# Attention, two feed-forward networks, one core: the first group of tokens becomes the first 192 of both batches

## The chip, the cores and the metric

The kernel runs on 1 core of one Trainium2 chip. Its engines are TensorE (PE, with its weight loads listed apart as PEld), VectorE (DVE), ScalarE (ACT), GpSimd (POOL) and SyncE (SP), whose queue issues all DMAs here. The metric is the device time of one execution in microseconds; the median of several runs counts. A change of about half a per cent is the least that is told apart.

## The reference, cut to what matters

```python
B, H, S, D = (2, 8, 576, 64)
scores = q @ k.T / sqrt(D), causal; a = softmax(scores); local = a @ v
q_p = where(q > 0, q, exp(q) - 1) + 1
mem_out = (q_p @ M_prev) / (q_p . z_prev + 1e-6)
x = g * mem_out + (1 - g) * local            # 1152 tokens (b, s) of 512
x = elu(x @ w_in) @ w_out                    # 512 -> 2048 -> 512
out = sum_e p[:, e] * (relu(x @ w1[e]) @ w2[e])   # 4 experts, 512 -> 1024 -> 512
```

All is float32. The weights of the first network come as float64.

## The kernel before, in words

Products of 32-bit accuracy are made of three matmuls on parts: each operand is split in a high part (ACT) and a low part (its remainder, POOL or DVE), and high x high, high x low and low x high are summed in PSUM (`mm3`, lines 249 to 252).

The 1152 tokens go through the two networks in two groups. Group 0 has 384 tokens (`NTOK`, line 254 on), group 1 has 768 and a second scheme with fewer products (`Wide`, line 661), which needs four differences of token quarters, T1 to T4 (`Halves.plan`, lines 630 to 658): a subtraction on DVE, a high part on ACT (`high`), a low part on POOL (`low`, L651), each in two halves kk. This is done twice: on the attention's output x ahead of the first network of group 1, and on its result y ahead of the second. Both are called junctions below.

Attention comes in 16 units, one per batch b, part and pair of heads c (`plan_unit`, line 1026). Part A has the query tiles from 64 to 448, which see 192, 320 and 448 keys; part B the tile from 448 to 576, which sees all 576, and the first 64 queries, doubled to fill a tile. A unit loads queries and keys, splits them (`split_h` on ACT, `split_l` on POOL, L1057), makes phi(q) for the memory part (`phi_r`, `phi_e` on ACT, `phi_p`, `phi` on POOL), and multiplies it with the memory (`mem`, L1108, one product per tile and head into bank o). The scores of the two heads are made side by side, in 64 rows of the array each (`score`, L1146, six matmuls for one piece of keys); DVE masks them, negates and finds the lowest (`lowest`, L1154); ACT makes the exponentials; 128 x 128 blocks are turned on PE (`transposes`, L1202), copied out of PSUM by ACT or DVE in turn (`evac`, L1208 and L1210) and multiplied with the values (`values`, L1217 for a full block, L1224 for the diagonal half blocks of both heads). DVE scales both parts (`quotient`, `times`, L1089 and L1095), POOL adds them (`both`, L1256), PE turns the sum (`turn`, L1262), and ACT and DVE write its parts to x (`join`, L1271 and L1273) or a plain copy (`join_w`, L1276).

The order on every engine is written out ahead by a planner (`Plan.order`, line 955): each step has an engine, an assumed cost, a rank (when it is due, in assumed us), steps it comes after, and buffers that it takes and gives back. A free engine takes the ready step of lowest rank. There are 13 matmuls on zeros first, to fill the time of the first loads (`WARM`). The four units 0A of group 0 are due 5 us apart; the layers' clock starts at `START2` = 60; the other twelve units are due at `START2` plus the entries of `STARTS2`, and run beside the networks of group 0:

```python
    GATE = ("0A3", "score10")
    START2 = 60.0
    STARTS2 = [30, 66, 74, 86, 97, 108, 119, 130, 141, 152, 163, 174]
    units = [(b, part, c) for b, part in ((0, "B"), (1, "A"), (1, "B")) for c in range(H // 2)]
```

The first network's 16 weight tiles arrive as float64 and are made float32 beside it (`plan_weights`, line 161): per half of a tile ACT scales the upper words into a PSUM bank s0 or s1 (`upper`, L193), and DVE shifts, joins and signs in three passes over 512 columns (L197, L201, L207). These two banks are those that the scores of all units use, so `upper` waits for `GATE`, a score of the last of the units 0A. Then the tile is split (L217 on ACT, L221 on POOL) and kept in DRAM for group 1.

Of the kernel before, what the change touches and what calls it, by code (L numbers as in the profile page):

```python
# [20 lines left out]
P = 128  # L21
NPART = 4
Q0 = [0, 64, 192, 320, 448]

QR = [128] * 5
EXT = [64, 192, 320, 448, 576]


PARTS = "AB"
TILES = {"A": [3, 2, 1], "B": [4, 0]}  # L30
KEYS = {"A": 448, "B": 576}
QCOLS = {"A": 384, "B": 256}
TCOLS = {"A": 384, "B": 192}
QCOL = {"A": {1: 0, 2: 128, 3: 256}, "B": {4: 0, 0: 128}}
FULL = {"A": 3, "B": 4}

BLOCKS = {
    part: [b for i in tiles for b in [(i, odd, j) for odd in (0, 1) for j in range(i)] + [(i, 2, i)]]
    for part, tiles in TILES.items()
}  # L40
# [3 lines left out]
ROWS = [[(0, 64 + P * t, P)] for t in range(3)] + [  # L44
    [(0, 448, P)],
    [(0, 0, D), (D, S + 448, D)],
    [(0, S + 512, D), (D, S, D)],
] + [[(0, S + 64 + P * t, P)] for t in range(3)]
TOKENS = {(0, "A"): (0, 0), (0, "B"): (1, 0), (1, "B"): (1, 192), (1, "A"): (1, 384)}
# [7 lines left out]
def tile_kernel(  # L57
    ctx: ExitStack,
    tc: tile.TileContext,
    qk_a: bass.AP,  # L60
    qk_b: bass.AP,
    vm_a: bass.AP,
    vm_b: bass.AP,
# [7 lines left out]
    qk, vm = {"A": qk_a, "B": qk_b}, {"A": vm_a, "B": vm_b}  # L71
# [21 lines left out]
    zeros = const.tile([P, 512], mybir.dt.bfloat16, name="zeros")  # L93
# [25 lines left out]
    def setup_probs():  # L119
# [9 lines left out]
    W_STEP = 6.0  # L129
    W_FIRST = 5  # L130
    NW = 5
    SLOTS = {
        "raw": 2, "rv": 2, "qh": 2, "ql": 2, "pe": 1, "pp": 2, "pt": 2, "nm": 4, "nr": 4, "tm": 2, "tv": 1,
# [27 lines left out]
    def plan_weights(plan, i, rank):  # L161
# [62 lines left out]
        if k < NW1 and not second:  # L224
            ends = []
            for half in range(2):
                last[0] = None
                add(f"load{half}", "sync", 1.6, lambda half=half: load64(half), [f"w64_{half}"])
                plan.add(
                    ("w", i, f"upper{half}"), "act", act_cost(512), rank, lambda half=half: upper(half),  # L230
                    [last[0], GATE] + [("w", i, "upper0")] * half, [f"s{half}"] + ["wr"] * (half == 0),
# [7 lines left out]
                    [f"w64_{half}", f"s{half}"],  # L239
# [47 lines left out]
    class Moe1:  # L287
# [26 lines left out]
        def before_up(self, part, fc):  # L314
            if part or self.g:
                return [], []
            return [(f"0A{c}", "join_l") for c in range(H // 2)], []
# [27 lines left out]
        def act(self, key, t, n):  # L345
            def exp():
                ev = hp[0].tile([P, 512], F32, tag="ev", name="ev" + "".join(map(str, key)), bufs=SLOTS["ev"])
                t["ev"] = ev[:, :n]
                nc.scalar.activation(out=t["ev"], in_=t["ps"], func=AF.Exp)
# [253 lines left out]
    class Halves:  # L603
# [26 lines left out]
        def plan(self, plan, rank, ready):  # L630

            for name, x, y in (("T1", "B12", "B11"), ("T2", "B22", "T1"), ("T3", "B22", "B12"), ("T4", "B21", "T2")):
                for kk in (0, 1):
# [16 lines left out]
                    def low(name=name, kk=kk):  # L650
                        nc.gpsimd.tensor_tensor(  # L651
# [7 lines left out]
                    plan.add(key(name, "l"), "pool", pool_cost(384), rank, low, [key(name, "h")], [], ["t32"] * kk)  # L659
# [278 lines left out]
    class Plan:  # L938
# [4 lines left out]
        def __init__(self, slots):  # L943
            self.steps, self.slots = {}, slots

        def add(self, key, engine, cost, rank, fn, after=(), takes=(), gives=(), slack=0.0):


            self.steps[key] = (engine, cost, rank, fn, after, takes, list(gives), slack)

# [4 lines left out]
        def order(self, free=None):  # L955
# [32 lines left out]
            while any(queues.values()):  # L988
# [27 lines left out]
                if not moved:  # L1016
                    times = [x + y for x in (*free.values(), *ends.values()) for y in slacks if x + y > now]
                    assert times, f"no step can start: {[q[:3] for q in queues.values()]}, {rings}"
# [4 lines left out]
    def segments(i):  # L1023
        return [(0, EXT[i])] if EXT[i] <= 512 else [(0, 288), (288, 576)]

    def plan_unit(plan, b, part, c, start, spare, slack):

        tiles, nt, nq, nk = TILES[part], len(TILES[part]), QCOLS[part], KEYS[part]
        slot = {i: n for n, i in enumerate(tiles)}
        base = {i: sum(EXT[x] for x in tiles[:n]) for n, i in enumerate(tiles)}  # L1030
        width = sum(EXT[i] for i in tiles)
        widest, entries = 960, 2 * FULL["B"] + 3
        unit, uid = {}, f"{b}{part}{c}"

        def add(key, engine, cost, fn, after=(), takes=(), gives=()):
            kind = key.rstrip("0123456789")
            plan.add(
                (uid, key), engine, cost, start + OFFSET[kind], fn,
                [(uid, a) if isinstance(a, str) else a for a in after], takes, gives, slack.get(engine, 0.0),
            )  # L1040


        def load():
            unit["k"] = atile([P, KEYS["A"] + QCOLS["A"]], F32, tag="raw", name=f"qk{uid}")[:, :nq + nk]
            nc.sync.dma_start(out=unit["k"], in_=qk[part][b, c])

        def load_v():
            unit["rv"] = atile([P, entries, DV], F32, tag="rv", name=f"rv{uid}")[:, :2 * FULL[part] + nt + 1]
            nc.sync.dma_start(out=unit["rv"], in_=vm[part][b, c])
# [351 lines left out]
```

## Time and profile before

| what | value |
|---|---|
| median of 3 runs | 754.3 us (753.38 to 756.7) |
| the profiled execution | 756.79 us |
| its span, first to last instruction | 755.0 us |
| PE busy | 730.8 us, 97% of the span |
| DVE, ACT, POOL busy | 422.7, 363.2, 443.9 us |
| mean granted clock of TensorE | 0.975 |

Matmuls overlap in the records: one of 384 columns is told as 0.34 us long, and the next starts after half of that. So the distance between starts, not the length, tells what PE can do. In a row of the timeline a first number is the start, the second the time from the first start to the last end; "x12" counts the instructions in it, and the bracket tells how long the engine was idle before, and what ended that.

### The profile page before, as it was taken

The page shows a single profiled execution, that of the slowest core. Times are in us where ns is not written, and L with a number is a line of the kernel's source. Part 1 is how long each engine was busy: PE and PEld are TensorE (multiplying, and loading weights), DVE is VectorE, ACT ScalarE, POOL GpSimd, SP SyncE. Part 2 cuts the span into 40 slices and gives each one's busy share as a digit, 9 for nine tenths or more (in the row PEclk, how much of TensorE's full clock was granted, in tenths as well). Part 3 has the DMA queues.
Part 4 walks back from the last instruction along what each step waited for, and adds up shares of the span by engine and source line. Part 5 has one row for each costly group of instructions (what it writes and reads, how often), then busy time and mean ns, then how long its engine had stood idle before and what let it go on. Part 6 is the DMA issues. An engine that isn't in the chain of part 4 may idle for free.

```text
span 755.0 us, 11115 instructions
## 1 busy us (share of the span) xinstructions
PE 730.8 (97%) x4205; PEld 656.1 (87%) x4205; DVE 422.7 (56%) x919; ACT 363.2 (48%) x639; POOL 443.9 (59%) x273
## 2 busy tenths in 40 slices
PE   9979898999999999999899999979999999999997
PEld 5868798888888888888799999969989889899896
DVE  4588879634534444443663674885546355364562
ACT  5657856855444354453475573853333234232220
POOL 5646656885574375454998655676456565665210
PEclk9968989999999999999899999989999999999999
DMA  6249878664253342330232131202213122032002
GB/s 239 82 142 317 285 237 269 216 210 118 75 154 92 102 127 66 113 113 29 99 100 94 63 107 50 63 28 85 84 29 111 37 77 84 28 112 56 1 0 84
DMA packets 24709, 82.61 MB, mean 109 GB/s; under 512 B 3024, under 2 KB 3024, under 8 KB 24656
## 3 DMA queue, kind: packets, MB, share of 16 engines
q1 hardware_dynamic: 24656, 81.91, 34.4%
q8 instruction: 33, 0.54, 0.3%
q14 instruction: 20, 0.16, 0.1%
HBM read 71.15 MB, written 10.75 MB: 108 GB/s over the span
## 4 chain that ended last, share of the span: by engine, by line
PE 85%; DVE 8%; ACT 2%; issue 2%; POOL 2%; DMA 1%; SPq 0%; DVEq 0%; POOLq 0%; ACTq 0%
PE db L250 9%; PE db L252 9%; PE db L251 9%; PE ub L250 4%; PE da L250 3%; PE da L252 3%; PE da L251 3%; PE ub L252 3%; PE ub L251 3%; PE o0A L1217 2%; DVE cv L201 2%; DVE cv L197 2%; PE o1A L1217 1%; DVE wr L207 1%; DVE yT L642 1%
## 5 line engine op out<-in xcount | busy, mean ns | idle before, releaser
L221 POOL TENSOR_TENSOR wl<-wr,wh 128x1024 fp32r<-128x1024 f32 x72 | 171.9, 2395 | 128.1 <-ACT wh L217 125.8
L217 ACT ACTIVATE wh<-wr 128x1024 fp32r<-128x1024 f32 x72 | 75.6, 1056 | 107.8 <-PE db L251 71.7
L250 PE MATMUL db<-wh,hb 128*128 128x512 f32 x288 | 115.8, 402 | 0.0
L252 PE MATMUL db<-wl,hb 128*128 128x512 f32 x288 | 112.8, 392 | 0.0
L251 PE MATMUL db<-wh,hb 128*128 128x512 f32 x288 | 112.6, 391 | 0.0
L899 DVE SCALAR_TENSOR_TENSOR acc<-db,pr,acc 128x512 f32<-128x512 f32 x42 | 31.5, 751 | 70.9 <-PE db L252 70.9
L250 PE MATMUL da<-ha,wh 128*128 128x384 f32 x192 | 66.1, 344 | 1.3 <-DVE xr L400 1.2
L252 PE MATMUL da<-ha,wh 128*128 128x384 f32 x192 | 65.4, 340 | 0.8 <-POOL ha L364 0.8
L251 PE MATMUL da<-ha,wl 128*128 128x384 f32 x192 | 65.1, 339 | 0.5 <-POOL wl L221 0.5
L252 PEld LDWEIGHTS db<-wl,hb 128*128 128x128 f32 x288 | 54.1, 188 | 11.8
L250 PEld LDWEIGHTS db<-wh,hb 128*128 128x128 f32 x288 | 54.1, 188 | 11.4 <-issue 0.5
L251 PEld LDWEIGHTS db<-wh,hb 128*128 128x128 f32 x288 | 54.2, 188 | 9.9
L250 PE MATMUL ub<-yh,wh 128*128 128x384 f32 x128 | 47.0, 367 | 0.0
L252 PE MATMUL ub<-yl,wh 128*128 128x384 f32 x128 | 43.2, 337 | 0.0
L251 PE MATMUL ub<-yh,wl 128*128 128x384 f32 x128 | 42.9, 335 | 0.0
L463 DVE SCALAR_TENSOR_TENSOR hb<-ub,hb 128x384 fp32r<-128x384 f32 x32 | 17.8, 556 | 38.2 <-ACT hb L460 38.1
L250 PEld LDWEIGHTS da<-ha,wh 128*128 128x128 f32 x192 | 36.6, 191 | 2.6 <-DVE xr L400 1.6
L252 PEld LDWEIGHTS da<-ha,wh 128*128 128x128 f32 x192 | 36.5, 190 | 1.9 <-POOL ha L364 1.7
L251 PEld LDWEIGHTS da<-ha,wl 128*128 128x128 f32 x192 | 36.6, 191 | 0.8 <-POOL wl L221 0.8
L460 ACT ACTIVATE hb<-ub 128x384 fp32r<-128x384 f32 x32 | 15.7, 491 | 32.9 <-PE ub L252 32.6
L490 DVE SCALAR_TENSOR_TENSOR acc<-db,pr,acc 128x512 f32<-128x512 f32 x21 | 15.7, 750 | 21.0 <-PE db L252 21.0
L250 PEld LDWEIGHTS ub<-yh,wh 128*128 128x128 f32 x128 | 24.1, 188 | 2.6 <-issue 1.5
(944 smaller groups left out, 1959.2 us busy)
## 6 DMA issues: line engine op xcount, KB each, us to landing
wr<-in_w SPq DMA_DIRECT2D x64, 512.0 KB, 3.7
w<-in_w SPq DMA_DIRECT2D x32, 512.0 KB, 5.7
wscr<-wr SPq DMA_DIRECT2D x16, 512.0 KB, 6.5
wr<-wscr SPq DMA_DIRECT2D x16, 512.0 KB, 3.4
out<-acc SPq DMA_DIRECT2D x7, 256.0 KB, 2.0
qk0A<-in_qk_a SPq DMA_DIRECT2D x4, 416.0 KB, 4.5
qk0B<-in_qk_b SPq DMA_DIRECT2D x4, 416.0 KB, 3.8
qk1A<-in_qk_a SPq DMA_DIRECT2D x4, 416.0 KB, 3.7
```

The source lines that it names most:

```text
L197: nc.vector.tensor_scalar(out=c, in0=c, scalar1=3, scalar2=None, op0=ALU.logical_shift_left)
L201: nc.vector.scalar_tensor_tensor(out=c, in0=low, scalar=29, in1=c, op0=ALU.logical_shift_right, op1=ALU.bitwise_or)
L217: nc.scalar.activation(out=t["wh"], in_=t["wr"], func=AF.Copy)
L221: nc.gpsimd.tensor_tensor(out=wl, in0=t["wr"], in1=f32(t["wh"]), op=ALU.subtract)
L250: nc.tensor.matmul(out, ah, bh, start=first, stop=False)
L251: nc.tensor.matmul(out, al, bh, start=False, stop=False)
L252: nc.tensor.matmul(out, ah, bl, start=False, stop=last)
L460: nc.scalar.activation(out=t["h"][:, 0], in_=t["ps"], func=AF.Relu)
L463: nc.vector.scalar_tensor_tensor(out=t["h"][:, 1], in0=t["ps"], scalar=0.0, in1=f32(t["h"][:, 0]), op0=ALU.max, op1=ALU.subtract)
L490: nc.vector.scalar_tensor_tensor(out=acc, in0=t["ps"], scalar=p, in1=acc, op0=ALU.mult, op1=ALU.add)
L899: nc.vector.scalar_tensor_tensor(out=acc, in0=t["ps"], scalar=p, in1=acc, op0=ALU.mult, op1=ALU.add)
L1217: nc.tensor.matmul(unit["ov"][:r, odd, slot[i]], pf[:, col:col + r], unit["rv"][:, odd * FULL[part] + (i - 1 - j if odd else j)], start=j ...
```

## The change

Group 0 is now the first 192 tokens of both batches. Attention has four units F, one for each pair of heads, for both batches: tiles 64 to 192 of batch 0 and of batch 1, which see 192 keys, and one tile that holds the first 64 queries of both batches. The scores of this third tile are two products into one bank, with zero columns in place of the other batch. F adds the two terms of phi in PSUM (two memory products) and makes max(q, 0) on ACT, so POOL has neither `phi_p` nor `phi` there; the first F unit's `split_l` is on DVE. Eight units R (batch, pair of heads) with the three tiles from 192 to 576, which see 320, 448 and 576 keys, come beside the layers, and no step of theirs may start more than 4 us ahead of its rank. The first weight tile is converted in banks m and doesn't wait for the gate. The low parts of T1 to T4 are on DVE for kk = 1. The rows of the output and of the second network's factors are ordered to match.

```diff
+QCOLS = {"F": 448, "R": 384}
+TILES = {"F": [(64, 192), (64, 192), (0, 64)], "R": [(448, 576), (320, 448), (192, 320)]}
+KEYS = {"F": 192, "R": 576}
+ROWS = [[(0, 64, P)], [(0, S + 64, P)], [(0, 0, D), (D, S, D)]] + [
+    [(0, S * b + 192 + P * t, P)] for b in (0, 1) for t in range(3)
+]
...
-    W_STEP = 6.0
+    W_RANKS = [12.0, 26.0, 32.0, 38.0, 44.0]
+    W_EARLY = 1
-        ... "tm": 2, ...
+        ... "tm": 1, ...
-    GATE = ("0A3", "score10")
+    GATE = ("F3", "score20")
+    EARLY = 4.0
-    START2 = 60.0
-    STARTS2 = [30, 66, 74, 86, 97, 108, 119, 130, 141, 152, 163, 174]
+    START2 = 48.0
+    STARTS2 = [12, 45, 75, 95, 110, 125, 140, 155]
...
-            t["cv", half] = abank(f"s{half}", f"cv{i}_{half}")
+            t["cv", half] = abank("m" if i < W_EARLY else f"s{half}", f"cv{i}_{half}")
...
-                    [last[0], GATE] + [("w", i, "upper0")] * half, [f"s{half}"] + ["wr"] * (half == 0),
+                    [last[0]] + [GATE] * (i >= W_EARLY) + [("w", i, "upper0")] * half, [bank] + ["wr"] * (half == 0),
...
                     def low(name=name, kk=kk):
-                        nc.gpsimd.tensor_tensor(
+                        eng = nc.vector if kk else nc.gpsimd
+                        eng.tensor_tensor(
...
-                        if not can_take(takes) or any(takers.get(x, [key])[0] != key for x in takes):
+                        if self.first[key] > now + 1e-6 or not can_take(takes) or any(takers.get(x, [key])[0] != key for x in takes):
...
+        def parts_of(t):
+
+            if kind == "F":
+                return [(t, 0, P)] if t < 2 else [(0, 0, D), (1, D, D)]
+            return [(0, 0, P)]
...
+            eng = nc.vector if uid == "F0" else nc.gpsimd
+            eng.tensor_tensor(out=unit["l"], in0=unit["k"], in1=f32(unit["h"]), op=ALU.subtract)
...
+            if kind == "F":
+                nc.scalar.activation(out=unit["phi"], in_=unit["k"][:, :nq], func=AF.Relu)
...
+            for t in range(nt):
+                for bi, r0, r in parts_of(t):
+                    q = qcol[t] + 2 * r0
+                    for odd in (0, 1):
+                        rows = slice(D * odd, D * odd + D)
+                        terms = ("e", "phi") if kind == "F" else ("phi",)
+                        for x in terms:
+                            nc.tensor.matmul(
+                                unit["om"][r0:r0 + r, odd, t], unit[x][rows, q:q + r],
+                                unit["rv"][rows, MEMORY[kind] + bi], start=x == terms[0], stop=x == terms[-1],
+                            )
...
         for i in range(WARM):
             ps = at["t"].tile([P, 512], F32, tag="t", name=f"warm{i}")
-            nc.tensor.matmul(ps, zeros[:, :P], zeros, start=True, stop=True)
+            nc.tensor.matmul(
+                ps.rearrange("p (n k) -> p n k", n=4), zeros, zeros.unsqueeze(1).to_broadcast([P, 4, P]), start=True, stop=True
+            )
...
         for c in range(H // 2):
-            plan_unit(plan, 0, "A", c, UNIT1 * c, True, {})
+            plan_unit(plan, "F", None, c, UNIT1 * c, True, {})
...
-        units = [(b, part, c) for b, part in ((0, "B"), (1, "A"), (1, "B")) for c in range(H // 2)]
+        units = [(b, c) for c in range(H // 2) for b in (0, 1)]
```

## Rows read from the trace of the kernel before

**Rows 1.** Stretches: length, busy us of PE, PEld, DVE, ACT, POOL, clock, DMA.

```profile
9.39:43.85 34.46, 31.99 (x291) 27.91 (x290) 22.44 (x79) 24.43 (x49) 20.50 (x16) 1.00 0.40 141
43.85:56.43 12.58, 10.49 (x54) 9.57 (x55) 10.11 (x20) 5.93 (x10) 5.76 (x6) 0.51 0.46 143
56.43:148.70 92.27, 85.06 (x475) 79.44 (x473) 76.17 (x150) 64.34 (x115) 60.63 (x39) 0.94 0.82 272
148.70:364.10 215.40, 215.40 (x1411) 184.37 (x1409) 91.10 (x275) 99.43 (x171) 124.99 (x75) 1.00 0.36 108
364.10:382.00 17.90, 15.37 (x68) 13.53 (x67) 14.81 (x20) 10.43 (x20) 16.85 (x12) 0.81 0.31 103
382.00:495.50 113.50, 113.50 (x656) 113.30 (x655) 70.44 (x138) 72.64 (x137) 79.10 (x45) 1.00 0.24 75
495.50:512.00 16.50, 12.27 (x51) 10.71 (x50) 13.02 (x19) 8.57 (x18) 12.69 (x11) 0.79 0.11 35
```

**Rows 2.** Timeline of PE among the units 0A, 30 to 45 us.

```profile
31.31 0.47 PE L1146 MATMUL s0A<-qh0A 64*128 64x448 f32 x2
...
32.10 0.89 PE L1108 MATMUL o0A<-rv0A,pp0A 64*128 64x65 f32 x12
33.20 0.55 PE L1262 MATMUL x0A<-ident,tv0A 128*128 128x128 f32 x3 [0.22 <-POOL tv0A L1256]
33.59 0.93 PE L1202 MATMUL t0A<-ident,pt0A 128*128 128x128 f32 x7
34.35 1.45 PE L1217 MATMUL o0A<-rv0A,pf0A 128*128 128x65 f32 x12
35.73 0.44 PE L1224 MATMUL o0A<-rv0A,pf0A 64*128 64x65 f32 x4
...
38.84 0.34 PE L1146 MATMUL s0A<-qh0A 64*128 64x192 f32 x2
...
39.34 1.09 PE L1202 MATMUL t0A<-ident,pt0A 128*128 128x128 f32 x8
```

**Rows 3.** Timeline of PE, a score piece of 64 columns and what follows.

```profile
91.25 0.30 PE L1146 MATMUL s0B<-qh0B 64*128 64x64 f32 x2 [2.09 <-DVE wr L207]
...
91.70 0.99 PE L1202 MATMUL t0B<-ident,pt0B 128*128 128x128 f32 x4
```

**Rows 4.** Timeline of DVE: evacuation, scores, quotient, next scores; one half tile's conversion.

```profile
31.91 0.68 DVE L1208 COPY pf0A<-t0A 128x512 f32<-128x512 f32 x1
32.51 0.61 DVE L1154 CUSTOM_DVE_ANT_0 pt0A<-s0A,mask 128x448 f32<-128x448 f32 x1
...
33.05 0.16 DVE L1089 SCALAR_TENSOR_TENSOR nm_0A<-o0A,wmem 128x6 f32<-128x6 f32 x1
...
33.95 0.61 DVE L1154 CUSTOM_DVE_ANT_0 pt0A<-s0A,mask 128x448 f32<-128x448 f32 x1
...
40.96 0.69 DVE L197 TENSOR_SCALAR cv<-cv 128x512 int32<-128x512 int32 x1
...
43.02 0.69 DVE L197 TENSOR_SCALAR cv<-cv 128x512 int32<-128x512 int32 x1
```

**Rows 5.** The stretch from the first weight conversion to the last, columns as rows 1.

```profile
40.96:137.80 96.84, 86.16 (x474) 80.00 (x474) 84.09 (x158) 64.77 (x118) 59.91 (x39) 0.88 0.76 251
```

**Rows 6.** Groups of PE's attention instructions, 56.43 to 148.7 us.

```profile
L1202 PE MATMUL t0B<-ident,pt0B 128*128 128x128 f32 x18 | 3.2, 303 | 0.0
...
L1217 PE MATMUL o0B<-rv0B,pf0B 128*128 128x65 f32 x16 | 2.8, 336 | 0.0
```

**Rows 7.** Timeline of PE at the two junctions, the waits for T2.

```profile
370.82 0.44 PE L252 MATMUL pa10S<-xT2l,swh48S 128*128 128x384 f32 x1 [2.04 <-POOL xT2l L651]
...
503.97 0.45 PE L250 MATMUL pb10S<-yT2h,swh64S 128*128 128x384 f32 x1 [3.62 <-ACT yT2h L648]
```

**Rows 8.** Timeline of DVE and of POOL at the second junction.

```profile
493.65 2.50 DVE L642 TENSOR_TENSOR yT<-xr 128x384 f32<-128x384 f32 x1 [1.44 <-ACT xr L822]
...
493.34 2.40 POOL L221 TENSOR_TENSOR wl<-wr,wh 128x1024 fp32r<-128x1024 f32 x1
```

More of the change, by code (lines that the diff above doesn't have):

```diff
@@ L92, in tile_kernel @@
         )
-    zeros = const.tile([P, 512], mybir.dt.bfloat16, name="zeros")
+    mask2 = const.tile([P, 2, D], F32, name="mask2")
+    nc.gpsimd.memset(mask2, 0.0)
+    for odd, step in ((0, -1), (1, 1)):
+        for half in (0, 1):
+            rows = mask2[D * half:D * half + D, odd]
+            nc.gpsimd.affine_select(
+                out=rows, in_=rows, compare_op=ALU.is_ge, fill=-8.0e9, base=-(D - 1) * odd,
+                pattern=[[step, D]], channel_multiplier=1,
+            )
+    zeros = const.tile([P, P], mybir.dt.bfloat16, name="zeros")
     nc.vector.memset(zeros, 0.0)
@@ L1017, in order @@
                     times = [x + y for x in (*free.values(), *ends.values()) for y in slacks if x + y > now]
+                    times += [self.first[key] for q in queues.values() for key in q if self.first[key] > now + 1e-6]
                     assert times, f"no step can start: {[q[:3] for q in queues.values()]}, {rings}"
@@ L1020, in order, with segments @@
             return free
[L1023 to L1033, printed above, removed]
+    def segments(ext):
+        return [(0, ext)] if ext <= 512 else [(0, 288), (288, 576)]
@@ new lines, in plan_unit @@
+    def plan_unit(plan, kind, b, c, start, spare, slack):
+        tiles, qcol, nkeys, full, nq = TILES[kind], QCOL[kind], KEYS[kind], FULL[kind], QCOLS[kind]
+        nt, nk = len(tiles), NBATCH[kind] * KEYS[kind]
+        base = [sum(ext for _, ext in tiles[:t]) for t in range(nt)]
+        width = sum(ext for _, ext in tiles)
+        widest, entries = 1344, ENTRIES["R"]
+        unit, uid = {}, f"F{c}" if kind == "F" else f"R{b}{c}"
+        def parts_of(t):
+            if kind == "F":
+                return [(t, 0, P)] if t < 2 else [(0, 0, D), (1, D, D)]
+            return [(0, 0, P)]
@@ L1154, in lowest @@
+        def lowest(odd, t, n):
+            q0, ext = tiles[t]
+            a, z_ = segments(ext)[n]
+            w, nm, at_ = z_ - a, unit["nm"][odd], 2 * t
+            if len(parts_of(t)) > 1:
+                masked = mask2[:, odd]
+            else:
+                m0 = 0 if odd else 448 - q0
+                masked = mask[:, odd, m0 + a:m0 + z_]
             nc.vector.tensor_tensor_reduce(
-                out=row(odd, i)[:, a:z_], in0=unit["s", odd, i, n][:r, :w], in1=mask[:r, odd, m0 + a:m0 + z_],
@@ L1173, in plan_unit, with expo @@
-        for i, n, a, z_ in pieces:
+                out=row(odd, t)[:, a:z_], in0=unit["s", odd, t, n][:, :w], in1=masked,
+                scale=-0.125, scalar=3.0e38 if n == 0 else nm[:, at_:at_ + 1],
+                op0=ALU.add, op1=ALU.min, accum_out=nm[:, at_ + n:at_ + n + 1],
+            )
+        def expo(odd, t):
+            k = 2 * t + len(segments(tiles[t][1])) - 1
+            blk = row(odd, t)
+            nc.scalar.activation(out=blk, in_=blk, func=AF.Exp, scale=-1.0, bias=unit["nm"][odd][:, k:k + 1])
@@ L1174, in plan_unit @@
+        for t, n, a, z_ in pieces:
+            first, last = (t, n) == pieces[0][:2], (t, n) == pieces[-1][:2]
+            add(
+                f"score{t}{n}", "pe", 3 * (z_ - a) / 2400 + 0.2, lambda t=t, n=n: score(t, n),
+                ["split_l"] + ["score{}{}".format(*pieces[0])] * (not first), s_from[t, n] + ["pt", "nm", "nm"] * first, ["qh", "ql"] * last,
+            )
+        for t, n, a, z_ in pieces:
             for odd in (0, 1):
                 add(
-                    f"lowest{i}{n}{odd}", "dve", dve_cost(z_ - a) + 0.12,
@@ L1186, in plan_unit @@
                 )
-        blocks = BLOCKS[part]
+        blocks = BLOCKS[kind]
         groups = [blocks[g:g + 4] for g in range(0, len(blocks), 4)]
```

279 lines of the change are left out of this document (135 added, 144 removed).

## The prediction

> **What bounds the kernel now.** I read the stretches first [rows 1]; the reader should see three stages ahead of 364.1 us and a packed rest. TensorE (PE) starts attention at 9.39 and the layers at 56.43. From there to 148.7 runs the first network on the first 384 tokens: PE is busy 85.06 of 92.27 us, and VectorE (DVE) 76.17. From 148.7 to 364.1 PE has no idle time. After that only attention's results are used, and what the change touches there are the two junctions (364.1 to 382, 495.5 to 512). So the end moves by what the 364.1 moves, plus the junctions.
>
> A busy PE is not a PE at its peak, so I count work by start-to-start distances in the first attention stage [rows 2]. Six score products of 192 columns take 0.50 (38.84 to 39.34), of 448 columns 0.79 (31.31 to 32.10), of 64 columns 0.45 [rows 3]; those of 288 and 320 lie between, about 0.61 and 0.64. Twelve memory products take 0.88 (32.10 to 33.20 less 0.22 idle), 0.073 each; a transpose 0.109 (33.59 to 34.35 for 7); a full-row value product 0.115 (34.35 to 35.73 for 12); a half-row one 0.11 (four in 0.44); the three of the last turn 0.39. The records hold two instructions per memory or value product.
>
> An old A unit is then 1.93 (scores) + 0.88 + 15 x 0.109 + 24 x 0.115 + 12 x 0.11 + 0.39 = 8.9 us. Four are 35.7, in a stage of 47.0 us (9.39 to 56.43). Up to 43.85 the units fill 30.5 of 34.46 us, or 0.885 (the last unit's 7 transposes, values and turn, 5.2 us, come later). The tail, 12.58 us, runs at a granted clock of 0.51: half of its matmuls' time is the clock, the rest 2.2 us of waiting. PE bounds this stage, with DVE busy 22.44.
>
> In the next stage DVE sets the pace. Every half tile of the first network's weights costs it three passes, 2.06 us from one start to the next (40.96 to 43.02) [rows 4]; 32 halves are 65.9 of the 84.09 us that it is busy between the first and the last of them [rows 5]. It is idle for only 12.7 there. PE waits in that stretch: 2.09 us for a score bank that conversion holds [rows 3]. Of PE's 92.27 us, 384 products of 0.173 us are 66.4 (the packed stretch has 656 in 113.50 us [rows 1]), and attention is about 9: 18 of the 0B units' 40 transposes and 16 of their 64 full-row value products [rows 6]. The other 17 us are waits and half clock.
>
> **The change, part by part.** *The early units.* Unit F has 7 blocks where A had 15, so 7 transposes and 8 full-row value products. Scores: two tiles of 192 columns and one of 64 done twice, 2 x 0.50 + 2 x 0.45 = 1.90. Half-row values: 16 x 0.11. But memory, now without the sum on GpSimd (POOL), multiplies two terms, and the shared tile does so per batch: 16 products, 32 instructions. Their price isn't in the trace in this shape: two in a row use the same half of the rows. Bounds are 0.055 (the shared tile's outputs are half as long) and 0.115 (no overlap, as a full-row product); I take 0.073, 2.34 us, since the rows are halves as before. F is 1.90 + 2.34 + 0.76 + 0.92 + 1.76 + 0.39 = 8.1 us, 7.5 to 9.4. Four are 32.3 against 35.7: PE is hardly relieved. POOL loses two passes per unit and ScalarE gains one; both were idle a quarter of that stage or more [rows 1], so I cost these at nothing, as I do the first unit's low parts on DVE.
>
> At the same filling, the units up to the last transposes take (32.3 - 3.4) / 0.885 = 32.7 us, so to 42.1; the tail has 3.4 us of work in place of 5.2, at half clock 6.8 + 2.2 = 9.0. The layers start at 51 in place of 56.4 (48 if the clock holds).
>
> *Units beside the layers.* R has 1344 score columns in four pieces, 21 blocks, 36 full-row value products: 2 x 0.61 + 0.79 + 0.64 + 0.88 + 2.29 + 4.14 + 1.32 + 0.39 = 11.7 us; eight are 93.4. What they replace: four A (35.7) and eight B (1.67 + 0.58 + 1.09 + 1.84 + 0.88 + 0.26 = 6.3 each), 86.3 together. PE gets 7.1 us more there and 3.4 less before.
>
> *DVE in the first network.* The first conversion tile moves ahead of the gate into spare banks, 2 x 2.06 us that DVE has free among the F units. The gate now is the last F unit's last score. Before, the first conversion started 15.5 us ahead of the layers; with the shorter tail I put it 12 ahead, at 39 in place of 40.96. DVE's work from there: 30 halves, 61.8; the network's own 23 passes of about 0.47, 10.8; the end of the last F unit, 2.6; and two R units, due at 12 and 45 us after the layers' start, in place of some 1.4 B units (7.4). An R unit on DVE: 0.54 per 448 score columns and in proportion, two heads, about 3.5; two evacuations of 0.60 and a short one, 1.35; two quotients with products of 0.90; two joins of 0.47 [rows 4]: 7.6. The sum is 90.4 against 84.1. With 10 us idle (I choose less than 12.7, because a DVE wait is more often filled by another unit; 5 to 12.7) the last conversion ends at 39 + 100.4 = 139.4 against 137.8, and the second network starts at 150.3. PE fits: 99 us for 66.4 + 23.4.
>
> *The second network.* What is left beside it shrinks from 86.3 - 9 - 0.6 = 76.7 to six R, 70.0. Its 215.4 become 208.7, and 364.1 becomes 359.0: 5.1 us earlier.
>
> *The junctions.* Half of the eight low parts go from POOL to DVE. PE idles 2.04 us for POOL's part at the first, 3.62 at the second for a high part [rows 7]; the second hangs on DVE, not on POOL. One such DVE pass took 2.50 beside a POOL pass of 2.40 [rows 8]. I take 1.5 and 0.2 gained; bounds +3 lost and -6 (both waits in full).
>
> The Trainium skill (SBUF — State Buffer, section "SBUF: two separate sides") says that a DVE pass with two SBUF inputs and a POOL pass that reads SBUF lock each other out for a whole instruction. The row of 2.50 agrees; by that rule each new low pass can also wait for a weights pass, which is the third rival.
>
> The Trainium skill (TensorEngine Tiling (Array Packing), section "Key Properties") says that a change of tiling mode drains TensorE. No row here shows a 64 x 64 product, as the shared tile's would be; by the rule the F units would be dearer by an estimated few tenths of a us each, inside the 9.4 above.
>
> *Costed at nothing.* The scaled memory part loses its second buffer (`tm`), so the next unit's waits for POOL's sum of the one before; bank o, which has one buffer, already makes that unit's memory products start after the sum's first input is out, and those products (2.3 us here) cover POOL's pass. If they don't, DVE stands behind it in its fixed order, and at most four passes are late ahead of the layers. Loads shrink by some bytes and keep their queue (SP), whose transfers are hidden in that stage, the fullest in DMA at 0.82 [rows 1]; the smaller zeros tile leaves 13 warm matmuls as they were.
>
> **Sum.** -5.1 - 1.7 = -6.8 us. The profiled execution took 756.79 (span 755.0 and 1.8 around it), 2.5 above the median of 754.3; I apply the difference to the median: 747.5. The forecast's own range, with 5 to 12.7 us idle, F at 7.5 to 9.4 and the junctions' nearer bounds, is 739 to 755.
>
> **The rivals.** *PE fills* (0.14): with R units at hand PE never waits for weights, the clock holds, the layers start at 48. For: the 17 us lost in the first network [rows 1]. Against: DVE's work there grows. The second network without attention is 215.4 - 76.7 = 138.7, so it ends at 48 + 66.4 + 93.4 + 138.7 = 346.5; with 1.7 from the junctions 735.
>
> *The F unit is no cheaper* (0.18): the same-row memory products and the small tile cost 9.4, the start stays at 55 to 56, and the 7 us more of R are absorbed by the 17: 754.
>
> *Lock at the junctions* (0.11): DVE's low passes stand behind POOL's 2.4 us weights passes; the junctions lose 1 each instead of gaining: 750.5.
>
> *Slower: DVE starves the weights* (0.15). An R step may start at most 4 us ahead of its rank, so R's passes come in bursts, and each of its four score pieces holds both banks that conversion writes. For: PE already waited 2.09 us at such a handover. Against: two R units have eight pieces, not many more than now. With 22 us of idle DVE, the last conversion ends at 151.4, the second network starts at 162.3 and ends at 371, and with nothing from the junctions it is 761. It decides from 19 us on.
>
> **How the numbers follow.** The forecast has 0.42. About 0.5% (3.8 us) is what a measurement here can tell from no change. Faster: 0.40 of the forecast, 0.14, half of the third rival, 0.01 of the second, 0.60 in all. Same: 0.02, 0.17, 0.05 and 0.02 of the last, 0.26. Slower: 0.14. The range 737 to 758 leaves out most of the slower case and about half of the fastest.
>
> **What would show it.** Right: the first layer product at 48 to 52, F units 8 us apart; the last weight conversion at 136 to 142; two R units' value products before the second network; the second part's first product near 359. Wrong: DVE idle by over 19 us among the conversions (slower), F memory products at 0.115 (same), a first layer product before 46 (faster than told), or junctions that change by more than 3 us.

## The result and the profile after

The changed kernel takes 765.49 us (median of 4, 764.65 to 766.11) against 754.67 (753.38 to 756.70): a ratio of 1.014, 95% interval 1.0115 to 1.0166. It is slower by 1.4%; 747.5 was forecast. Ratios here leave out disturbed executions, medians and ranges do not.

The profiled execution took 766.11 us, with a span of 764.3. Its stretches, cut where those of before are cut [rows 1] (length, then busy us of PE, PEld, DVE, ACT, POOL, then granted clock, DMA share, GB/s):

```profile
9.20:20.00 10.80, 10.79 (x86) 9.68 (x86) 4.11 (x24) 6.66 (x16) 3.30 (x2) 1.00 0.56 185
20.00:57.74 37.74, 35.09 (x276) 30.29 (x277) 20.59 (x68) 15.98 (x34) 8.93 (x7) 0.99 0.28 88
57.74:155.66 97.92, 89.84 (x530) 81.99 (x529) 80.75 (x157) 70.46 (x123) 69.10 (x42) 0.95 0.75 264
155.66:370.71 215.05, 215.05 (x1395) 186.62 (x1394) 87.34 (x230) 96.16 (x148) 113.73 (x62) 1.00 0.30 100
370.71:389.00 18.29, 13.57 (x58) 11.57 (x57) 17.71 (x23) 10.24 (x20) 15.14 (x10) 0.81 0.41 130
504.00:521.00 17.00, 11.93 (x51) 10.78 (x50) 15.83 (x22) 8.56 (x18) 9.56 (x7) 0.80 0.27 86
```

The edges of the stretches give the account of the 9.3 us between the two spans:

| | before | after | difference | foretold |
|---|---|---|---|---|
| attention ahead of the layers, to | 56.43 | 57.74 | +1.3 | -5.4 |
| first network, group 0, long | 92.27 | 97.92 | +5.7 | +7.0 |
| second network, group 0, long | 215.40 | 215.05 | -0.4 | -6.7 |
| from group 1's first product to the end | 390.9 | 393.6 | +2.7 | -1.7 |

Three of the four stages went wrong, and the one that got longer as foretold did so with less work in it than foretold. I take them in turn.

**The early units run at half clock.** PE's timeline among the F units (start, length, engine, line, operation, tiles, count):

```profile
14.56 1.75 PE L1252 MATMUL tF<-ident,ptF 128*128 128x128 f32 x7
16.25 0.53 PE L1194 MATMUL sF<-qhF 64*128 64x192 f32 x2
16.57 0.41 PE L1194 MATMUL sF<-qlF,qhF 64*128 64x192 f32 x2
16.79 0.41 PE L1194 MATMUL sF<-qhF,qlF 64*128 64x192 f32 x2
```

Two rows of the kernel before, of the same shape:

```profile
39.02 0.28 PE L1146 MATMUL s0A<-ql0A,qh0A 64*128 64x192 f32 x2
39.13 0.28 PE L1146 MATMUL s0A<-qh0A,ql0A 64*128 64x192 f32 x2
```

Seven transposes from 14.56 to the next start at 16.25 are 0.24 each; they were 0.109 [rows 2]. A pair of 192 columns follows the one before after 0.22, where before it was 0.11. Both are twice the time. Yet the clock column of the windows above reads 1.00 and 0.99: the trace's clock record begins only at 53.3 us in this execution, and a column without a record reads 1.00. What tells the clock here is the pitch: 1.2 GHz, not 2.4, up to 53.3 us, while PE is busy 10.79 of the first 10.80 us. The third tile's scores of successive units start at 13.14, 21.61, 32.72 and 40.91: a unit every 9.26 us.

The conversion that the gate should release at 39 waits for this too. DVE's timeline at the end of the stage:

```profile
46.43 0.16 DVE L1126 SCALAR_TENSOR_TENSOR nv_F<-oF,wloc 128x6 f32<-128x6 f32 x1 [3.56 <-PE oF L1275]
47.88 0.69 DVE L213 TENSOR_SCALAR cv<-cv 128x512 int32<-128x512 int32 x1
```

ACT had filled both banks by 44.3, but in DVE's fixed order the conversion stands behind a quotient, which waits 3.56 us for PE's slow value products.

**Only one R unit runs in the first network.** Groups of PE between 57.7 and 155.7 us (busy, mean ns, idle before):

```profile
L1266 PE MATMUL oR<-rvR,pfR 128*128 128x65 f32 x36 | 4.8, 273 | 0.0
L1252 PE MATMUL tR<-ident,ptR 128*128 128x128 f32 x21 | 3.4, 281 | 0.6 <-ACT pfR L1259 0.4 <-ACT ptR L1217 0.2
```

21 transposes and 36 full-row values are one unit's; two units' scores (48 records) and memory products are there, but the second unit's blocks are turned and multiplied only beside the second network, which is why that is hardly shorter.

**The junction waits for DVE.** DVE, POOL and PE at the first junction:

```profile
376.06 0.55 DVE L669 TENSOR_TENSOR xT2l<-xT,xT2h 128x384 fp32r<-128x384 f32 x1
377.00 3.98 DVE L659 TENSOR_TENSOR xT<-x,xT 128x384 f32<-128x384 f32 x2
381.37 0.88 DVE L669 TENSOR_TENSOR xT3l<-xT,xT3h 128x384 fp32r<-128x384 f32 x1
382.63 2.27 DVE L669 TENSOR_TENSOR xT4l<-xT,xT4h 128x384 fp32r<-128x384 f32 x1
```

```profile
377.89 2.67 POOL L237 TENSOR_TENSOR wl<-wr,wh 128x1024 fp32r<-128x1024 f32 x1
381.79 2.69 POOL L237 TENSOR_TENSOR wl<-wr,wh 128x1024 fp32r<-128x1024 f32 x1
```

```profile
382.30 0.69 PE L269 MATMUL pa10S<-xT3l,swh48S 128*128 128x384 f32 x1 [3.05 <-DVE xT3l L669]
```

Two subtractions take 3.98 us beside POOL's 2.67 of weights; the low part of T3 comes behind them, and PE waits 3.05 for it. T4's own pass takes 2.27 beside the next 2.69; a pass that meets none takes 0.55. The Trainium skill (SBUF — State Buffer, section "SBUF: two separate sides") says of such a pair that whichever starts first keeps the other out for its whole length; these rows agree.

### The profile page after: what moved, and what is told of

Its sections match the earlier page's. It is cut to its first block, busy times and chain, and to the rows that moved or that the text cites. A ratio compares the mean times of both kernels' runs of the same rounds, so it can differ in the third digit from the quotient of the medians.

```text
span 764.3 us, 11115 instructions
## 1 busy us (share of the span) xinstructions
PE 738.2 (97%) x4261; PEld 663.5 (87%) x4261; DVE 422.7 (55%) x884; ACT 358.9 (47%) x615; POOL 415.7 (54%) x245
## 4 chain that ended last, share of the span: by engine, by line
PE 85%; DVE 8%; ACT 2%; issue 2%; DMA 1%; POOL 1%; DVEq 0%; SPq 0%; ACTq 0%
PE db L267 9%; PE db L269 9%; PE db L268 9%; PE oR L1266 4%; PE ub L267 3%; PE da L269 3%; PE da L267 3%; PE da L268 3%; PE ub L269 3%; PE ub L268 3%; PE tR L1252 3%; PE sR L1194 2%; PE sF L1194 2%; DVE cv L217 2%; PE oF L1148 1%
## 5 line engine op out<-in xcount | busy, mean ns | idle before, releaser
L918 DVE SCALAR_TENSOR_TENSOR acc<-db,pr,acc 128x512 f32<-128x512 f32 x42 | 31.5, 751 | 71.0 <-PE db L269 71.0
L269 PEld LDWEIGHTS db<-wl,hb 128*128 128x128 f32 x288 | 54.1, 188 | 11.7
L1266 PE MATMUL oR<-rvR,pfR 128*128 128x65 f32 x288 | 37.5, 271 | 0.0
L1217 ACT ACTIVATE ptR<-ptR,nmR 128x576 f32<-128x576 f32 (+2 forms) x48 | 30.3, 662 | 15.0 <-DVE nmR L1208 15.0
L1266 PEld LDWEIGHTS oR<-rvR,pfR 128*128 128x128 f32 x288 | 35.5, 192 | 1.0 <-issue 0.2
```

Of the source, the lines that this page charges most:

```text
L269: nc.tensor.matmul(out, ah, bl, start=False, stop=last)
L918: nc.vector.scalar_tensor_tensor(out=acc, in0=t["ps"], scalar=p, in1=acc, op0=ALU.mult, op1=ALU.add)
L1217: nc.scalar.activation(out=blk, in_=blk, func=AF.Exp, scale=-1.0, bias=unit["nm"][odd][:, k:k + 1])
L1266: nc.tensor.matmul(unit["ov"][:, odd, t], pf[:, col:col + P], unit["rv"][:, at_], start=j == 0, stop=False)
```

## The experiments

e1, e2, e3 and e5 start from the changed kernel, e6 is e2 and e3 together, e7 to e10 start from e6, e11 from e10, e12 from the kernel before. "Layers", "second" and "group 1" are the starts of the first product of the first network, of the second, and of group 1, in the profiled execution; "rest" is from there to the end.

| kernel | median (range) us | ratio [95%] | layers | second | group 1 | rest |
|---|---|---|---|---|---|---|
| before | 754.67 (753.38 to 756.70) | | 56.4 | 148.7 | 364.1 | 390.9 |
| after | 765.49 (764.65 to 766.11) | 1.014 [1.0115, 1.0166] | 57.7 | 155.7 | 370.7 | 393.6 |
| e1 | 765.52 (765.09 to 765.75) | 1.0131 [1.0111, 1.0151] | 59.1 | 155.9 | 370.9 | 392.4 |
| e2 | 761.29 (757.41 to 776.46) | 1.0082 [1.0051, 1.0113] | 49.0 | 146.2 | 361.2 | 394.4 |
| e3 | 762.33 (760.65 to 762.60) | 1.0085 [1.0063, 1.0107] | 55.6 | 153.5 | 368.5 | 390.3 |
| e5 | 769.98 (768.49 to 770.60) | 1.0188 [1.0165, 1.0210] | 62.3 | 158.9 | 373.4 | 393.3 |
| e6 | 758.19 (753.64 to 773.03) | 1.0031 [1.0002, 1.0060] | 53.2 | 150.9 | 366.0 | 390.3 |
| e7 | 753.35, one execution | | 54.5 | 152.4 | 362.2 | 389.3 |
| e8 | 774.96 (764.62 to 775.41) | 1.0217 [1.0163, 1.0270] | 65.7 | 166.7 | 383.5 | 389.7 |
| e9 | 767.07 (761.28 to 773.09) | 1.0119 [1.0057, 1.0182] | 60.2 | 148.5 | 379.6 | 391.5 |
| e10 | 756.22 (754.11 to 763.32) | 1.0035 [1.0003, 1.0068] | 51.1 | 148.9 | 364.0 | 389.2 |
| e11 | 757.12 (755.87 to 765.09) | 1.0039 [1.0012, 1.0067] | 61.7 | 159.2 | 374.3 | 389.0 |
| e12 | 756.76 (753.39 to 759.76) | 1.0005 [0.9982, 1.0028] | 57.0 | 145.9 | 361.4 | 390.5 |

The kernel before had, in the runs beside e1 to e5, a median of 755.45, beside e6 to e9 756.42, beside e10 to e12 756.10 (751.74 to 759.59).

The clock record of the profiled executions first shows 2.4 GHz at 13.4 us in before, and at 53.3 in after, 62.1 in e1, 41.0 in e3 and 65.8 in e5; with zero matmuls among the F units at 10.9 in e2, 21.4 in e6 and 12.7 in e10. In after, e1 and e3, which have the same work ahead of the layers, the layers start the later the later the clock comes up (55.6, 57.7 and 59.1 for 41.0, 53.3 and 62.1).

**e1: the warm matmuls' operand.** The diff changed it to a broadcast; here it is plain again.

```diff
+        wide = atile([P, 3, 2, D], F32, tag="tv", name="wide").rearrange("p a b d -> p (a b d)").bitcast(mybir.dt.bfloat16)[:, :512]
+        nc.vector.memset(wide, 0.0)
...
-            nc.tensor.matmul(
-                ps.rearrange("p (n k) -> p n k", n=4), zeros, zeros.unsqueeze(1).to_broadcast([P, 4, P]), start=True, stop=True
-            )
+            nc.tensor.matmul(ps, wide[:, :P], wide, start=True, stop=True)
```

> The changed kernel with the 13 warm matmuls read from a plain 512-column tile of zeros, as before the change; nothing else. Theory (the F units' own short matmuls keep TensorE at its lower clock): no difference, transposes of the F units still 0.26 us each, first layer product at 57 to 58, 765 us. Rival (reading one small tile over and over made the warm matmuls too light to raise the clock): the clock rises near 13 us as in the kernel before, transposes fall to 0.11, first layer product near 49 to 51, 755 to 758 us.

765.52 us and the layers at 59.1: nothing gained, as the theory had it. The low clock isn't the warm matmuls' doing.

**e2: wide zero matmuls among the F units**, 24 in all, into banks that the scores then overwrite.

```diff
             for odd in (0, 1):
                 tag = "m" if "m" in s_from[t, n] else f"s{odd}"
                 unit["s", odd, t, n] = abank(tag, f"s{uid}{odd}{t}{n}")
+                if kind == "F":
+                    nc.tensor.matmul(
+                        unit["s", odd, t, n].rearrange("p (n k) -> p n k", n=4), zeros,
+                        zeros.unsqueeze(1).to_broadcast([P, 4, P]), start=True, stop=True,
+                    )
```

> The changed kernel with one matmul on zeros of 512 columns ahead of each score product bank of the F units (24 in all); it writes a bank that the scores then overwrite. Theory (short matmuls keep the clock low in the F units, and that costs 8 to 9 us up to the gate): the clock rises ahead of 25 us, later transposes of F take 0.11, the first layer product comes at 49 to 53 in spite of some 6 us of added matmuls, and the time is 757 to 761 us. Rival (the F stage is long for its waits, not for its clock): the added matmuls lengthen it to 62 or more, and the time is 768 to 772 us.

PE's timeline, and two stretches:

```profile
14.65 0.88 PE L1257 MATMUL tF<-ident,ptF 128*128 128x128 f32 x6
...
16.46 0.35 PE L1199 MATMUL sF<-qhF 64*128 64x192 f32 x2
16.65 0.28 PE L1199 MATMUL sF<-qlF,qhF 64*128 64x192 f32 x2
16.76 0.27 PE L1199 MATMUL sF<-qhF,qlF 64*128 64x192 f32 x2
```

```profile
20.00:48.97 28.97, 24.80 (x284) 18.34 (x284) 20.40 (x68) 15.96 (x35) 9.01 (x7) 0.99 0.37 116
48.97:146.17 97.20, 89.22 (x531) 80.76 (x529) 80.75 (x157) 70.36 (x123) 69.13 (x42) 0.97 0.76 265
```

With *more* work on PE the layers start 8.8 us earlier and group 1 9.5 earlier. A pair of scores follows after 0.11 again; the clock record has 2.4 GHz from 10.9 to 48.4 us. So the clock is what made the stage slow: shown. The first network, though, is as long as ever, 97.20 us. And the gain isn't there in every execution: the profiled one is the shortest of six, and the median gained 4.2 us (765.49 to 761.29).

**e3: all low parts of T1 to T4 on POOL again.**

```diff
-                        eng = nc.vector if kk else nc.gpsimd
+                        eng = nc.gpsimd
...
-                    eng = ("dve", dve_cost(384)) if kk else ("pool", pool_cost(384))
+                    eng = ("pool", pool_cost(384))
```

> The changed kernel with all low parts of T1 to T4 on GpSimd again. Theory (DVE's low passes stand in the way of its own subtractions, and behind GpSimd's weights passes): the time from the first product of the second part to the end goes from 393.6 to about 391 us, 762.5 us in all. Rival (the difference behind 370.7 us has another cause, such as where the weights passes fall): 393.6 stays, 765 us.

The rest falls from 393.6 to 390.3, just under the 390.9 of before: this part of the change costs 3.3 us. The other runs bear it out: the rest is 392.4 to 394.4 in the four profiles with low parts on DVE (after, e1, e2, e5) and 389.0 to 391.5 in the seven of this grouping without. The two longest of PE's six waits at the first junction are now

```profile
374.41 0.44 PE L269 MATMUL pa10S<-xT2l,swh48S 128*128 128x384 f32 x1 [1.11 <-POOL xT2l L669]
375.69 0.44 PE L269 MATMUL pa10S<-xT2l,swh48S 128*128 128x384 f32 x1 [0.49 <-POOL xT2l L669]
```

and none reaches the 3.05 above; PE's named waits there are 2.95 us in all, against 4.72 after the change, and 4.24 against 5.08 at the second junction. (The 2 us that this execution also has ahead of the layers go with a clock record that starts at 41.0 instead of 53.3.)

**e5: R steps may start at any time.**

```diff
-    EARLY = 4.0
+    EARLY = 1e9
```

> The changed kernel without the bound of 4 us ahead of its rank for a step of an R unit. Theory (the first network is fed by weight conversion, so R cannot fill it): R units' early steps move ahead, first network to within 2 us of 98, total 763 to 767 us. Rival (the bound keeps R out of the first network, and TensorE waits there for nothing): two R units' value products come ahead of 155 us, the second network is 5 to 10 us shorter, 756 to 760 us.

4.5 us slower than the change, and above the theory's 763 to 767. Steps of R moved ahead of the layers (which start at 62.3), while the first network shrank by 1.2 (96.7) and the second by 0.6. The clock record begins at 65.8 here, so how much of the later start is the moved steps and how much the clock isn't separated. The first network still has one R unit's 36 full-row value products: the bound on R's steps isn't what keeps the second out of it.

**e6: e2 and e3 together.**

> The two earlier edits together: zero matmuls ahead of the score banks of the F units, and all low parts of T1 to T4 on GpSimd. Theory (clock in the F stage and DVE at the junctions are the two losses against the kernel before): first part ends at 361 as with the first edit alone, the rest takes 390.5 as with the second alone, 752 to 755 us, within half a per cent of the kernel before. Rival (the edits' gains overlap or the second was only a gain of its own run's first part): 757 or more.

Within 0.3% of before, with executions from 753.64 to 764.7 (and one at 773.03). The two causes hold nearly all of the loss. The median, 758.19, is still above the theory's 752 to 755 and in the rival's range; the rest fell to 390.3 as expected, and what is missing lies ahead of it (366.0 for 361), where the clock came up at 21.4 us instead of 10.9. But the kernel is no faster than before, though in e2 it reached the layers 7.5 us sooner. The next three start from e6 and ask where that goes.

**e7: the third conversion pass left out**, so that DVE has 32 passes less; the signs of the first network's weights are not set.

```diff
         def lower(half):
             c, low = t["cv", half].bitcast(I32), t[half][0]
+            wi = t["wr"][:, 512 * half:512 * half + 512].bitcast(I32)
             nc.vector.scalar_tensor_tensor(
-                out=c, in0=low, scalar=29, in1=c, op0=ALU.logical_shift_right, op1=ALU.bitwise_or
+                out=wi, in0=low, scalar=29, in1=c, op0=ALU.logical_shift_right, op1=ALU.bitwise_or
             )
...
-                ends.append(("w", i, f"sign{half}"))
+                ends.append(("w", i, f"lower{half}"))
```

> As the two edits together, but without the third DVE pass of the conversion (the sign of the first network's weights is left out), 32 passes of 0.69 us. Theory (DVE sets the pace of the first network): from the third half tile's conversion to the last it takes 75 to 83 us in place of 91 to 92, and the second network starts 8 to 15 us earlier. Rival (the DMA of the float64 weights, at a share of 0.76 in that stage, or the chain from one engine to the next sets it): less than 4 us.

Stretches of e6, then stretches and groups of e7:

```profile
53.18:150.94 97.76, 89.73 (x530) 81.92 (x529) 80.78 (x157) 70.39 (x123) 69.07 (x42) 0.95 0.76 264
150.94:366.00 215.06, 215.06 (x1395) 186.63 (x1394) 87.39 (x230) 96.27 (x148) 113.72 (x62) 1.00 0.31 100
```

```profile
54.53:152.40 97.87, 94.93 (x586) 87.19 (x585) 63.48 (x130) 72.58 (x127) 72.95 (x44) 0.98 0.80 274
152.40:362.20 209.80, 209.80 (x1337) 180.19 (x1337) 84.23 (x223) 91.60 (x140) 107.72 (x58) 1.00 0.29 94
```

```profile
L1271 PE MATMUL oR<-rvR,pfR 128*128 128x65 f32 x64 | 8.3, 271 | 0.0
L1257 PE MATMUL tR<-ident,ptR 128*128 128x128 f32 x41 | 6.4, 277 | 0.9 <-ACT pfR L1264 0.8
```

This is a single execution. The expected shorter network did not come: 97.87 us against 97.76, although the last conversion ends at 126.0 instead of 137.6 (86.7 us from the third half tile on, where 75 to 83 were expected), and the second network starts no earlier. What came is the second R unit: 41 transposes and 64 values in place of 21 and 36, PE busy 94.93, and a second network of 209.80, 5.3 us shorter. So less conversion on DVE lets more attention in beside the first network: the order written ahead turns free DVE time into attention, not into an earlier end.

**e8: three weight tiles converted ahead of the gate.**

```diff
-    W_RANKS = [12.0, 26.0, 32.0, 38.0, 44.0]
+    W_RANKS = [12.0, 17.0, 22.0, 38.0, 44.0]
...
-    W_EARLY = 1
+    W_EARLY = 3
```

> As the two edits together, but three weight tiles in place of one are converted ahead of the gate, in banks m, due at 12, 17 and 22. Theory (DVE's work from the gate on sets when the first network ends): 16 to 17 us of DVE work less the 8 that two tiles cost, last conversion some 6 us earlier, second network 4 to 7 us earlier, 746 to 751 us. Rival (DVE, ScalarE or the banks are then short among the F units): first layer product 4 us later or more, no gain.

```profile
20.00:65.74 45.74, 39.24 (x314) 28.47 (x313) 24.01 (x80) 21.38 (x44) 12.64 (x8) 0.66 0.33 105
65.74:166.75 101.01, 89.84 (x515) 82.94 (x514) 79.14 (x150) 70.74 (x120) 71.67 (x43) 0.94 0.75 257
```

Slower by 2.2%, with the rival's signs (layers 4 us later or more, no gain): the layers start at 65.7, at a clock of 0.66 (the record has 2.4 GHz from 20.6 to 34.2 us only). The edit hardly brought conversions forward: the third half starts at 50.8 (45.5 in e6), and six are begun ahead of the layers where e6 has five. So it doesn't test the theory. How much of the 12.6 us the conversions caused and how much the clock did isn't separated here.

**e9: no R unit due in the first network.**

```diff
-    STARTS2 = [12, 45, 75, 95, 110, 125, 140, 155]
+    STARTS2 = [70, 85, 100, 113, 126, 139, 152, 165]
```

> As the two edits together, with the R units due at 70, 85, 100, 113, 126, 139, 152, 165 in place of 12, 45, 75 and so on: none is due in the first network. Theory (the first network is paced by DVE, and an R unit in it costs DVE 7.6 us there, and saves TensorE 11.7 later): first network about 6 to 8 us shorter, second 10 to 12 longer, 2 to 5 us slower in all. Rival (TensorE has room, R in the first network is free): first network unchanged, 10 us slower. Second rival (R there costs as much as it saves): within 1 us.

The profiled execution took 773.09 us, at 0.73 of the clock ahead of the layers, and its first network has 0.89 of the clock where e6's has 0.95, so the lengths compare only roughly:

```profile
60.25:148.50 88.25, 77.92 (x386) 73.64 (x385) 70.24 (x115) 60.86 (x104) 60.35 (x36) 0.89 0.82 279
148.50:379.58 231.08, 231.08 (x1538) 199.47 (x1538) 98.30 (x271) 104.95 (x167) 120.68 (x67) 1.00 0.31 98
```

Against e6 the first network is 9.5 us shorter (97.76 to 88.25) and the second 16.0 longer (215.06 to 231.08). So attention beside the first network is not free: what it does there saves the second network 16.0 us of PE, and the first is some 9.5 longer for it, perhaps more at an equal clock. Nor can it be left out: the two together are 6.5 longer here, and the kernel's two shortest executions, 761.28 and 761.59, are 3.1 and 3.4 above e6's median, within the theory's 2 to 5.

**e10: a second zero matmul at each bank of the first F unit; e11: four more ahead of the last F unit's turn; e12: the kernel before with such matmuls in its last units' tail.**

```diff
-                if kind == "F":
+                for _ in range(2 if uid == "F0" else 1 if kind == "F" else 0):
...
             unit["x"] = abank(x_from, f"x{uid}")
+            for _ in range(4 * (uid == "F3")):
+                nc.tensor.matmul(
+                    unit["x"].rearrange("p (n k) -> p n k", n=4), zeros,
+                    zeros.unsqueeze(1).to_broadcast([P, 4, P]), start=True, stop=True,
+                )
```

```diff
             pst = unit["t", g] = abank(t_from[g], f"t{uid}{g}")
+            for _ in range(4 * (uid == "0A3")):
+                nc.tensor.matmul(pst, zeros[:, :P], zeros, start=True, stop=True)
...
             unit["x"] = abank(x_from, f"x{uid}")
+            for _ in range(4 * (uid in ("0A2", "0A3"))):
+                nc.tensor.matmul(unit["x"], zeros[:, :P], zeros, start=True, stop=True)
```

> As e6_dense_pool, with a second zero matmul ahead of each of the six score banks of the first F unit. In the profile of e6 the clock came up at 21.4 us, in that of e2 at 10.9 us, with the same work in the same order up to there; e6's runs went from 753.6 to 764.7 us. Theory (the spread is when the clock comes up): with more wide work at the start the clock is up at 10 to 14 us, the first layer product at 47 to 50 us, and the median at 752 to 755 us with a spread under 4 us. Rival (the spread is something else): the first layer product stays at 52 to 54 us, and the six matmuls add 2 to 3 us: 758 to 761 us.

> As e10_two_zeros, with four zero matmuls ahead of the last F unit's turn, in its bank, where TensorE waits 2.3 us in e2 for GpSimd's sum. Theory: they lie in the wait and keep the clock up, so that the first products of the first network go at full clock: 1 to 2 us less than e10, 750 to 754 us, below the kernel before (754 to 757). Rival: the clock falls for another reason, or the matmuls stand behind the wait: the same as e10 within 1 us.

> The kernel before (its grouping unchanged), with four zero matmuls ahead of each group of transposes of the last unit 0A and ahead of the turns of the last two, where TensorE waits 4.1 us between 40 and 56 us and its clock is half from 44.1 to 61.2 us. Theory (the clock's level is set by what TensorE does in those waits): the clock stays up, the stretch from 43.85 us to the first layer product shrinks from 12.6 to 8 to 10 us, and the time falls by 2 to 6 us, to 750 to 754 us. Rival (the tail is paced by VectorE and GpSimd): 24 matmuls of 0.26 us more and nothing gained: 755 to 761 us.

Neither made the clock sure. e10's executions lie at 754.1 to 757.2 (seven, mean granted clock 0.981 to 0.989) and at 762.3 to 763.3 (three, 0.969 to 0.975); e11's at 755.9 to 757.2 (seven, 0.981 to 0.990) and 761.9 to 765.1 (five, 0.969 to 0.972). A profile of each kind, e10's at 754.95 and e11's at 765.09 (the kernels differ by e11's four matmuls):

```profile
20.00:51.12 31.12, 26.94 (x306) 20.11 (x302) 21.32 (x75) 18.09 (x40) 10.26 (x7) 0.99 0.39 121
51.12:148.92 97.80, 91.15 (x531) 83.63 (x529) 81.05 (x157) 70.44 (x123) 69.02 (x42) 0.93 0.77 264
```

```profile
20.00:61.67 41.67, 39.86 (x307) 29.65 (x306) 21.36 (x75) 17.90 (x40) 10.25 (x7) 0.63 0.28 90
61.67:159.20 97.53, 90.49 (x531) 82.16 (x530) 81.12 (x157) 70.69 (x123) 69.08 (x42) 0.95 0.76 265
```

The difference, 10.5 us, lies ahead of the layers, where the second ran at 0.63 of the clock; after that they agree. e10's expectation failed (a spread under 4 us, layers at 47 to 50, a median of 752 to 755). Its reading of the spread held in part: the clock makes it, but not by when it comes up. It came up at 12.7 us in the first profile and at 12.6 in the second, and there fell again from 26.3 to 57.0. e11's four matmuls gained nothing over e10 that its spread lets one see.

e12 tells what a held clock is worth to the old grouping:

```profile
43.85:57.00 13.15, 9.66 (x67) 7.45 (x66) 10.23 (x20) 6.84 (x12) 7.10 (x5) 0.87 0.59 177
57.00:145.95 88.95, 80.19 (x475) 74.38 (x473) 75.77 (x149) 64.53 (x115) 59.04 (x39) 1.00 0.83 276
```

The tail's clock rises from 0.51 [rows 1] to 0.87, but the tail is no shorter (13.15 against 12.58), as the rival had it: 3.0 us of it are zero matmuls, and PE idles 3.5 where it idled 2.1. The network behind it is 3.3 us shorter in this execution, one of the four shortest of twelve. The median stays (ratio 1.0005), so no complete version here beats the kernel before.

## Why the prediction was wrong

*"PE bounds this stage", the early units' price.* This is the step that failed first: the clock that the F units would get. Every price was a pitch from [rows 2], at 2.4 GHz, and the half clock was allowed for in the tail alone ("48 if the clock holds" was put on the good side only). At full clock F is cheaper than the 8.1 us I gave it: in e2 the third tile's scores start at 13.86 and 36.59, 7.6 per unit, of which 1.6 are six zero matmuls of 0.27; 6.0 us are left, waits included. The layers then start at 49.0 in that profile, even with 24 zero matmuls in the way. At the clock that the chip granted, it is 9.26 and the layers start at 57.7 in place of 51. Memory products, the price I doubted, take 2.56 us per unit at half clock (10.58 to 13.14 in the profile after) and 1.46 in e2 (11.87 to 13.33), against 2.34: no matter.

*The gate at 39.* It opened in time for ACT to write the banks at 43, but DVE started at 47.88, for the same cause; in e2 at 41.28.

*DVE's sum of 90.4 and 10 idle.* From the first of these conversions to the last:

```profile
47.88:142.30 94.42, 84.06 (x491) 77.46 (x489) 79.06 (x145) 63.73 (x113) 59.76 (x38) 0.95 0.74 258
```

79.06 busy, and 15.4 idle, above the 12.7 that I took as the upper end. The 11 us less work is mostly the missing unit (7.6). That DVE sets the pace was right in part. On the chain of work that ended last, in the profile after, the three conversion passes hold 28.9% of the first network, the largest share of any engine but PE, and none lies behind 118.4 us. There the chain goes on with a load of weights (start, length):

```profile
118.45 7.53 DMA w<-in_w
```

and, from 126 us on, with ACT and PE. ACT waits 7.3 us for such loads (3.9 before), which the prediction costed at nothing. In e7's chain no conversion pass is left, and PE's products of the network hold 57.8%: with fewer passes the pace goes over to PE.

*"Two R units" beside the first network.* One ran, with the second's scores and memory products. By the prediction's own prices that is 11.7 + 2.65 + 0.88 = 15.2 us, and the second network should be 138.7 + 93.4 - 15.2 = 216.9; it was 215.05. With two there, 208.7; e7, which has nearly two, had 209.80. With none, 232.1; e9 had 231.08. So the sum's structure was right and its count wrong: this step is worth 6.3 us (215.05 against 208.7).

*The first network.* Foretold 150.3 - 51 = 99.3, measured 97.92: near, but by luck. The conversions took 94.4 us in place of 100.4 (one R unit instead of two), they began 9.9 us ahead of the layers in place of 12, and the network ended 13.4 behind the last one in place of 10.9. Its length scarcely depends on when it starts (96.7 to 97.9 in after, e1, e2, e3, e5, e6, e7, e10 and e11), and it is longer than that of before: in e10 a start 5.3 us earlier is followed by a network 5.5 longer. With the clock held and the low parts back on POOL, group 1 starts at 363.97 against 364.11: with its 30 zero matmuls, which no run with a held clock leaves out, the regrouping gains nothing there.

*The junctions.* I took 1.7 gained and measured 2.7 lost, 3.3 by e3. The rival named the mechanism (DVE's passes behind POOL's 2.4 us weights passes) but priced it at 1 a junction; the row of 2.50 [rows 8] was the price, several times over, and the bound of +3 was the right end. (By its own terms that rival comes to 754.3 - 5.1 + 2 = 751.2, not 750.5.)

*The sum of the misses:* 6.7 at the layers' start, -1.4 in the first network, 6.3 in the second, 4.4 behind: 16.0 of the 16.1 from 750.0 (756.79 less 6.8) to the profiled 766.11. The slower rival, at 761, had the sign and not the cause: DVE's idle time is under its 19 us, and setting the bound on R's steps aside (e5) made things worse. The rival in which the F unit is no cheaper had the late start, but put it on dearer products, not on the clock.

**What stays open:** which property of the F units' matmuls leaves the clock low from the start. Units 0A, of much the same operations with more blocks, longer score rows and no 64 x 64 product, have it from 13.4 to 44.1 us; in e10 and e11 the same kernel does both. Nor is it shown why the clock falls again in some executions. The losses of e5 and e8 aren't split between what was moved and the clock.

## What to carry to other kernels

Price TensorE's work at both of its clock levels and ask which the changed stage will have: a stage of short matmuls, mixed otherwise, can stay at half clock, and then less work takes longer; read the level from the pitch of known operations, because a clock column without records reads 1.00. When work is moved between stages that run beside each other, count what the pacing engine lets in at each place, since a freed pass may come out as more hosted work instead of an earlier end (e7). And the price of a pass moved to VectorE can be that of a pass beside GpSimd's long ones (here up to 2.3 us), not that of a pass alone (0.55).

## What the runs showed of the hardware

- PE was busy 10.79 of the first 10.80 us among the F units by its records, and its pitch was that of 1.2 GHz, there and on to 53 us. The Trainium skill (TensorE: Matmul & The Clock Gate, section "What's actually happening") has the clock set by how busy PE has been of late; here the records were as busy as they can be at the low level, so their busy time doesn't tell which level comes.
- 24 added matmuls made a stage shorter by 8.8 us in the profiled execution (e2).
- One kernel, two times: 754.1 to 757.2 and 762.3 to 763.3 us (e10), at a mean granted clock of 0.981 to 0.989 and 0.969 to 0.975. In the profiles of e10 and e11, one of each kind, the difference lies ahead of the layers.
- A product on 64 x 64 of the array was no dearer: the shared tile's 16 records per unit take 0.42 us in e2 (12.91 to 13.33), with 0.15 to 0.2 us lost at the change of shape (starts of groups of four records 0.37 to 0.40 apart where they are 0.22 otherwise), no more than the few tenths that the prediction estimated.
